# Tail products of four jobs on sixteen 32x32 tiles of TensorE at once, with the tails turned between partition quadrants by small SBUF copies

## Chip, cores and metric

The kernel runs on one core of one Trainium2 chip. The metric is the device time in microseconds (us); lower is better.

## The reference

```python
B, D, L = 16384, 416, 6                 # D = 26 * 16
# x0: (B, D), ws: (L, D, D), bs: (L, D), all bfloat16
def reference(x0, ws, bs):
    x = x0
    for l in range(L):
        proj = jnp.einsum('bd,de->be', x, ws[l]) + bs[l]
        x = x0 * proj + x
    return x
```

The rows are independent, so the kernel cuts them into 8 groups `g` of 2048 rows. One *job* is (g, l): one layer of one group. Its activations lie transposed in SBUF (the on-chip memory that the engines read), features on its 128 partitions. 416 features are three full tiles of 128 and a **tail** of 32. A row of the tail would waste three quarters of the 128 partitions, so the tail is folded: the 2048 rows are four chunks `j` of 512, and chunk j of the tail lies on partition quadrant j (partitions 32j to 32j+31) of one 128x512 tile.

## The kernel before

A job (g, l) makes 3 full output tiles (128 features x 2048 rows, 4 banks of PSUM, the memory in which TensorE sums) and one output tail (32 features x 4 chunks, one bank).

- `full`: 12 products 128x128, one per input tile and chunk.
- `rows32`: the contribution of the input tail to a full output tile. Four products with a contraction of only 32 rows, from the four quadrants, run side by side as tiles 32x128.
- `tails`: the output tails. The outputs have 32 features, so four products with 32 columns run side by side as tiles 128x32, one per chunk, each into its quadrant of the bank. The input tail's own share of the output tail would be 32x32; it is padded to 128 rows by a block-diagonal weight tile `wbd`.

```python
def rows32(g, l, i, banks, first):
    src, stok = x3_src(g, l)                              # the input tail, 128 x 512
    for j in range(NJ):
        q = slice(j * T32, (j + 1) * T32)
        ... matmul(bank(banks[j]), w3[l][q, ecols], src[q, :], tile_position=(j * T32, 0))

def tails(batch):                                         # up to four jobs, one bank each
    bs_ = take(len(batch))
    for (g, l), b in zip(batch, bs_):
        for t in range(NT):                               # three full input tiles
            for j in range(NJ):
                ... matmul(bank(b, j * T32, (j + 1) * T32), wm[l][:, t, NT * P:D], src(t, j, j + 1),
                           start=(t == 0), stop=False, tile_position=(0, j * T32))      # L449
        for j in range(NJ):                               # the input tail, padded
            ... matmul(bank(b, j * T32, (j + 1) * T32), wbd[l][:, j * T32:(j + 1) * T32], s3,
                       start=False, stop=True, tile_position=(0, j * T32))              # L454
        evacuate_tail(g, l, b)     # ScalarE: ts = psum + bias; VectorE: ts *= x0 tail; x3 = ts + old x3

def make_wbd(l):                                          # GpSimd builds the padding
    add("pool", memset(wbd[l], 0))
    for j in range(NJ): add("pool", tensor_copy(wbd[l][q, q], w3[l][q, NT * P:D]))
... # cut: loads, start, order of tiles, output, the last layer of the last group
```

Jobs run along antidiagonals of (g, l): a job's input comes from a job up to four places earlier (four for most jobs), and tails are made in batches. There are 47 tails in 14 batches: nine of four jobs, two of three, two of two and one of one. Each batch stands inside the stream of tiles.

## Time and profile before

| | before |
|---|---|
| time, median (range) | 487.95 us (487.85 to 488.16, 4 runs) |
| span, first to last instruction | 485.8 us |
| TensorE busy / VectorE / ScalarE | 99% / 84% / 71% |
| granted TensorE clock | 0.999 |
| TensorE waits for other engines, in all | 2.8 us |

The profile has its own short names: PE is TensorE, PEld its weight loads, DVE VectorE, ACT ScalarE, POOL GpSimd and SPq the queue of SyncE; L424 is line 424 of the kernel.

From the page of the kernel before: the span, the busy times, the chain that ended last by engine and by line, and the groups of the products and of the tails' VectorE add. Columns of a group are line, engine, operation, output and inputs, shape, count, then busy us and mean ns of one, then the idle time just before.

```profile
span 485.8 us, 8101 instructions
PE 478.7 (99%) x3253; PEld 203.4 (42%) x3253; DVE 407.8 (84%) x713; ACT 343.2 (71%) x372; POOL 16.5 (3%) x44
...
PE 96%; DVE 2%; ACT 1%; POOL 0%; issue 0%; POOLq 0%
...
L424 PE MATMUL ps<-x,wm 128*128 128x512 bf16 x1692 | 379.4, 380 | 0.0
...
L436 PE MATMUL ps<-x,w 32*128 32x512 bf16 x564 | 44.5, 380 | 1.0 <-DVE x L414 1.0
L449 PE MATMUL ps<-x,wm 128*32 128x512 bf16 x564 | 38.7, 380 | 0.0
...
L454 PE MATMUL ps<-x,wbd 128*32 128x512 bf16 x188 | 18.3, 379 | 0.0
```

The chain is TensorE almost alone, so the time is the sum of what TensorE has to issue. A matmul lasts 380 ns, but successive ones overlap: what counts is the distance of their starts. A busy TensorE therefore says nothing about how well its tiles are used. That is read from the timeline. The next lines are the timeline of TensorE in the kernel before, around one batch of four tails; columns are start (us), length (us), engine, line, operation and count.

```profile
158.80 0.40 PE L436 MATMUL ps<-x,w 32*128 32x512 bf16 x4
159.13 0.83 PE L449 MATMUL ps<-x,wm 128*32 128x512 bf16 x12
159.79 0.39 PE L454 MATMUL ps<-x,wbd 128*32 128x512 bf16 x4
160.00 0.82 PE L449 MATMUL ps<-x,wm 128*32 128x512 bf16 x12
160.65 0.39 PE L454 MATMUL ps<-x,wbd 128*32 128x512 bf16 x4
...
162.38 0.39 PE L454 MATMUL ps<-x,wbd 128*32 128x512 bf16 x4
162.70 0.60 PE L424 MATMUL ps<-x,wm 128*128 128x512 bf16 x2
```

From 160.00 to 160.65 there are 12 products in three rounds of four, 0.216 us a round; from 159.79 to 160.00 the padded L454 round costs as much as any other. The batch runs from 159.13 to 162.70: 3.57 us = 16 rounds x 0.216 + 0.11. The remainder 0.11 is at the end, where the tile shape changes from 128x32 to 128x128. It is the same at 158.80 to 159.13, where a round of 0.216 takes 0.33.

There is one more place where TensorE loses time, early on. Its timeline in the kernel before, near 24 us (the square bracket is idle time and what ended it):

```profile
23.15 0.40 PE L436 MATMUL ps<-x,w 32*128 32x512 bf16 x4
24.50 0.40 PE L436 MATMUL ps<-x,w 32*128 32x512 bf16 x4 [0.95 <-DVE x L414]
24.82 1.47 PE L424 MATMUL ps<-x,wm 128*128 128x512 bf16 x6
```

The second group of four reads the first tail that was computed, and has to wait for VectorE's add (L414) to write it.

### The profile page before, as it was taken

What the parts mean: (1) busy time and instruction counts of PE and PEld (TensorE: products, weight loads), DVE (VectorE), ACT (ScalarE), POOL (GpSimd) and SP (SyncE); (2) the same over time, 40 slices, a digit from 0 to 9 for tenths busy, and PEclk for the clock granted to TensorE, in tenths of its full rate; (3) what the DMA queues carried; (4) which work ended last, traced back from release to release, by engine and by line L of the source; (5) the groups of instructions that cost most, each with busy time, mean ns of one, the idle gap of its engine ahead of it and who ended that gap; (6) DMA issues with size and microseconds to landing.
All of it is one profiled execution on the core that took longest, in us unless ns stands there. A gap on an engine that the chain in (4) does not pass through costs nothing.

```text
span 485.8 us, 8101 instructions
## 1 busy us (share of the span) xinstructions
PE 478.7 (99%) x3253; PEld 203.4 (42%) x3253; DVE 407.8 (84%) x713; ACT 343.2 (71%) x372; POOL 16.5 (3%) x44
## 2 busy tenths in 40 slices
PE   8999999999999999999999999999999999999996
PEld 6344444444444444434444444444444444444353
DVE  2878888888888888888889888988888888888887
ACT  4567777677677676766777767767777767777775
POOL 1123000000000000000000000000000000000000
PEclk9999999999999999999999999999999999999999
DMA  8997860000002397269209911850000137027277
GB/s 228 203 186 168 169 139 1 0 1 0 2 1 43 67 239 119 45 149 229 46 13 203 227 24 36 214 175 1 1 1 1 24 67 193 0 45 169 73 160 260
DMA packets 126249, 47.65 MB, mean 98 GB/s; under 512 B 107002, under 2 KB 124804, under 8 KB 126212
## 3 DMA queue, kind: packets, MB, share of 16 engines
q1 hardware_dynamic: 125464, 46.60, 42.9%
q8 instruction: 25, 0.41, 0.4%
q10 hardware_dynamic: 748, 0.54, 0.3%
q14 instruction: 12, 0.10, 0.1%
HBM read 5.97 MB, written 13.63 MB: 40 GB/s over the span
## 4 chain that ended last, share of the span: by engine, by line
PE 96%; DVE 2%; ACT 1%; POOL 0%; issue 0%; POOLq 0%
PE ps L424 76%; PE ps L436 8%; PE ps L449 6%; PE ps L454 2%; PE ps L767 1%; PE ps L520 1%; PE ps L500 1%; DVE x L397 1%; ACT x L795 1%; DVE tw L392 1%; ACT x L759 0%; PE ps L525 0%; DVE x L802 0%; PE ps L778 0%; ACT tw L383 0%; PE ps L737 0%
## 5 line engine op out<-in xcount | busy, mean ns | idle before, releaser
L383 ACT ACTIVATE tw<-ps,bias 128x1024 bf16<-128x1024 f32 (+1 forms) x295 | 299.8, 1071 | 128.3 <-PE ps L436 104.5
L424 PE MATMUL ps<-x,wm 128*128 128x512 bf16 x1692 | 379.4, 380 | 0.0
L424 PEld LDWEIGHTS ps<-x,wm 128*128 128x128 bf16 x1692 | 158.9, 98 | 213.3 <-issue 28.5
L392 DVE TENSOR_TENSOR tw<-tw,x 128x1024 bf16<-128x1024 bf16 (+1 forms) x285 | 193.7, 685 | 62.9 <-ACT tw L383 62.5
L397 DVE TENSOR_TENSOR x<-tw,x 128x1024 bf16<-128x1024 bf16 (+1 forms) x285 | 182.6, 681 | 0.0
L436 PE MATMUL ps<-x,w 32*128 32x512 bf16 x564 | 44.5, 380 | 1.0 <-DVE x L414 1.0
L449 PE MATMUL ps<-x,wm 128*32 128x512 bf16 x564 | 38.7, 380 | 0.0
L410 ACT ACTIVATE ts<-ps,bias 128x512 bf16<-128x512 f32 x47 | 28.8, 700 | 0.0
L436 PEld LDWEIGHTS ps<-x,w 32*128 32x128 bf16 x564 | 9.1, 92 | 34.4 <-issue 33.1
L449 PEld LDWEIGHTS ps<-x,wm 128*32 128x32 bf16 x564 | 13.8, 96 | 15.7 <-issue 2.9
L609 POOL COPY ost<-ot 128x512 bf16<-128x512 bf16 x7 | 5.0, 717 | 412.9 <-DMA ot<-x 412.9
L414 DVE TENSOR_TENSOR x<-ts,x 128x512 bf16<-128x512 bf16 x47 | 18.5, 417 | 0.0
L412 DVE TENSOR_TENSOR ts<-ts,x 128x512 bf16<-128x512 bf16 x47 | 18.5, 417 | 0.0
L454 PE MATMUL ps<-x,wbd 128*32 128x512 bf16 x188 | 18.3, 379 | 0.0
L294 POOL COPY wbd<-w 32x32 bf16<-32x32 bf16 x24 | 9.3, 388 | 35.4 <-DMA w<-in_ws_dram 34.2
L767 PE MATMUL ps<-wm,x 128*128 128x416 bf16 x48 | 9.4, 341 | 0.0
L533 DVE COPY x<-ps 128x512 bf16<-128x512 bf16 x4 | 1.7, 424 | 8.6 <-PE ps L525 8.6
L795 ACT ACTIVATE x<-ps 128x416 bf16<-128x416 f32 x15 | 7.4, 530 | 1.3 <-PE ps L767 1.2
L530 ACT ACTIVATE x<-ps 128x512 bf16<-128x512 bf16 x8 | 4.3, 594 | 4.5 <-PE ps L520 4.5
L454 PEld LDWEIGHTS ps<-x,wbd 128*32 128x32 bf16 x188 | 5.0, 97 | 5.1
L767 PEld LDWEIGHTS ps<-wm,x 128*128 128x128 bf16 x48 | 5.1, 115 | 3.8 <-issue 1.4
L797 DVE TENSOR_TENSOR x<-x,x 128x416 bf16<-128x416 bf16 x15 | 5.5, 370 | 1.1 <-ACT x L795 1.0
(37 smaller groups left out, 49.7 us busy)
## 6 DMA issues: line engine op xcount, KB each, us to landing
out_dram<-ost SPq DMA_DIRECT2D x7, 1664.0 KB, 6.8
x<-in_x_dram SPq DMA_DIRECT2D x7, 416.0 KB, 7.5
wm<-in_ws_dram SPq DMA_DIRECT2D x5, 312.0 KB, 3.1
x<-Tb SPq DMA_DIRECT2D x28, 32.0 KB, 2.3
out_dram<-x SPq DMA_DIRECT2D x1, 832.0 KB, 3.6
w<-in_ws_dram SPq DMA_DIRECT2D x20, 26.0 KB, 2.2
x<-in_x_dram SPq DMA_DIRECT2D x2, 208.0 KB, 3.1
out_dram<-x SPq DMA_DIRECT2D x1, 416.0 KB, 2.5
```

The source lines that it names most:

```text
L383: add("act", lambda h, a=a, w=w, b0=b0: h.activation(tw[r][:, a * CH:(a + w) * CH], psum[:, b0 * CH:(b0 + w) * CH], ACT_F.Identity, bias=b ...
L392: add("dve", lambda h, a=a, e=e: h.tensor_tensor(tw[r][:, a * CH:e * CH], tw[r][:, a * CH:e * CH], x0s[s0][:, i * GC + a * CH:i * GC + e * ...
L397: add("dve", lambda h, a=a, e=e: h.tensor_tensor(xs[so][:, i * GC + a * CH:i * GC + e * CH], tw[r][:, a * CH:e * CH], src(i, a, e), ALU.ad ...
L410: add("act", lambda h: h.activation(ts[r][:, :], bank(b), ACT_F.Identity, bias=bias[:, 3, l:l + 1], scale=1.0), reads=[("ps", b), "bias"], ...
L412: add("dve", lambda h: h.tensor_tensor(ts[r][:, :], ts[r][:, :], x0s[s0][:, XW:XW + CH], ALU.mult), reads=[("ts", r)] + x03_toks(s0), writ ...
L414: add("dve", lambda h: h.tensor_tensor(x3s[so][:, :], ts[r][:, :], src, ALU.add), reads=[("ts", r)] + stok, writes=[("x3", so)], hold=True)
L424: add("pe", lambda h, t=t, j=j: h.matmul(bank(banks[j]), wm[l][:, t, ecols], src(t, j, j + 1), start=(first and t == 0), stop=(not first a ...
L436: add("pe", lambda h, q=q, j=j: h.matmul(bank(banks[j]), w3[l][q, ecols], src[q, :], start=first, stop=not first, tile_position=(j * T32, 0)),
L449: add("pe", lambda h, t=t, j=j, src=src, l=l, b=b: h.matmul(bank(b, j * T32, (j + 1) * T32), wm[l][:, t, NT * P:D], src(t, j, j + 1), star ...
L454: add("pe", lambda h, j=j, s3=s3, l=l, b=b: h.matmul(bank(b, j * T32, (j + 1) * T32), wbd[l][:, j * T32:(j + 1) * T32], s3, start=False, s ...
L767: add("pe", lambda h, t=t: h.matmul(bank(b, n=D), xcol(t, j, kk), wm[l][:, t, :], start=(first and t == 0), stop=(not first and t == NT - 1)),
L795: add("act", lambda h: h.activation(o, bank(b, n=D), ACT_F.Copy), reads=[("ps", b)], writes=extra + [("on", j, kk)])
```

## The change

The padded round does 32x32 of useful work in a 128x32 tile. The array can be cut in 16 tiles of 32x32, so the four padded rounds of a batch could be one round, **if the sixteen products of four jobs fall on sixteen distinct tiles**. Without more they do not: chunk j of every job lies on quadrant j and goes to quadrant j, so all jobs use the four diagonal tiles. The change therefore lets the tail of a group lie *turned*: for odd layers its chunks are moved by 0, 1, 1 or 2 quadrants according to g mod 4. Going from even to odd layers a job's product then moves by +0, +1, +1, +2 quadrants and from odd to even by -0, -1, -1, -2. Since neighbours in a batch differ by one in g and in l, four neighbours get the offsets 0, 1, 3 and 2, which are all different.

The price: `x3 = ts + old x3` needs the old tail in the new position. The new tail tile is filled beforehand with the turned old tail by two SBUF-to-SBUF DMAs, and the group's x0 tail gets a turned copy too. About 70 DMAs are added, all on the one queue (SyncE's) that also carries loads and outputs. `wbd` and its GpSimd work go. The early order of tiles changes too. To find memory for the turned copies, the transposed tail buffer `Tb` moves into the output buffer `ost`, and one temporary of the tails and a separate buffer of the biases are dropped. The core of the diff, cut:

```diff
-    NX0, NXS, NX3, NTW, NTS = 5, 6, 8, 4, 5
+    NX0, NXS, NX3, NTW, NTS = 5, 6, 10, 4, 4
...
-    def make_wbd(l): ...                               # and its calls
...
+        if turn_of(g, 1):                              # at the end of load_group
+            rotate(x0s[s][:, XW:XW + CH], x0s[s][:, XW + CH:XW + 2 * CH], turn_of(g, 1),
+                   x03_toks(s), ("x03r", s), f"x03r_{s}", g)
...
+    def turn_of(g, l):
+        return (0, 1, 1, 2)[g % 4] if l % 2 else 0
+    def quad(g, l, j):
+        q = (j + turn_of(g, l)) % NJ
+        return q, slice(q * T32, (q + 1) * T32)
+    def rotate(src, dst, n, reads, token, lane, batch):
+        a = P - n * T32
+        add("sp", lambda h: h.dma_start(dst[n * T32:P, :], src[0:a, :]), ...)
+        add("sp", lambda h: h.dma_start(dst[0:n * T32, :], src[a:P, :]), ...)
...
     def done_with(g, l):
...
+        prefill(g, l + 1)                              # turned copy of the old tail into the new
         if l == L - 1:
             output(g)
...
     def tails(batch):
         bs_ = take(len(batch))
+        for (g, l), b in zip(batch, bs_):
+            s3, tok3 = x3_src(g, l)
+            for j in range(NJ):
+                (ri, qi), (ro, qo) = quad(g, l, j), quad(g, l + 1, j)
+                add("pe", ... h.matmul(psum[qo, b * CH:(b + 1) * CH], w3[l][qi, NT * P:D], s3[qi, :],
+                    start=True, stop=False, tile_position=(ri * T32, ro * T32)), ...)
         for (g, l), b in zip(batch, bs_):
             for t in range(NT):
                 for j in range(NJ):
-                    ... matmul(bank(b, j * T32, (j + 1) * T32), ..., start=(t == 0), stop=False,
-                               tile_position=(0, j * T32))
+                    ... matmul(psum[qo, b * CH:(b + 1) * CH], ..., start=False, stop=(t == NT - 1),
+                               tile_position=(0, ro * T32))
-            for j in range(NJ):
-                ... matmul(bank(b, j * T32, (j + 1) * T32), wbd[l][:, j * T32:(j + 1) * T32], s3, ...)
...
-    where[((1, 0), 1)] = where.pop(((1, 0), 0))
-    tiles = [((1, 0), 0), ((0, 1), 0), ((1, 0), 1), ((0, 1), 1), ((0, 1), 2), ((1, 0), 2)]
+    where[((0, 1), 0)] = where.pop(((1, 0), 0))
+    tiles = [((1, 0), 0), ((1, 0), 1), ((0, 1), 0), ((0, 1), 1), ((0, 1), 2), ((1, 0), 2)]
```

More of the change, by code (lines that the diff above doesn't have):

```diff
@@ L234, in bass_standalone__cross_network_dcn__recsys_kernel @@
     w3 = [nc.alloc_sbuf_tensor(f"w3_{l}", [P, D], BF16) for l in range(L)]
-    wbd = [nc.alloc_sbuf_tensor(f"wbd_{l}", [P, P], BF16) for l in range(L)]
     ident = nc.alloc_sbuf_tensor("ident", [P, P], BF16)
     bias = nc.alloc_sbuf_tensor("bias", [P, 4, L], FP32)
-    bs_sb = nc.alloc_sbuf_tensor("bs_sb", [P, D], BF16)
     brow = nc.alloc_sbuf_tensor("brow", [P, D], BF16)
@@ L241, in bass_standalone__cross_network_dcn__recsys_kernel @@
     ones = nc.alloc_sbuf_tensor("ones", [P, P], BF16)
-    x0s = [nc.alloc_sbuf_tensor(f"x0_{s}", [P, XW + CH], BF16) for s in range(NX0)]
+    x0s = [nc.alloc_sbuf_tensor(f"x0_{s}", [P, XW + 2 * CH], BF16) for s in range(NX0)]
     xs = [nc.alloc_sbuf_tensor(f"x_{s}", [P, XW], BF16) for s in range(NXS)]
     x3s = [nc.alloc_sbuf_tensor(f"x3_{s}", [P, CH], BF16) for s in range(NX3)]
-    Tb = nc.alloc_sbuf_tensor("Tb", [P, GC], BF16)
     tw = [nc.alloc_sbuf_tensor(f"tw_{s}", [P, GC], BF16) for s in range(NTW)]
@@ L248, in bass_standalone__cross_network_dcn__recsys_kernel @@
     ost = nc.alloc_sbuf_tensor("ost", [P, GC // P, D], BF16)
+    Tb = ost[:, :, :].rearrange("p a f -> p (a f)")[:, 0:GC]
     ot3 = nc.alloc_sbuf_tensor("ot3", [P, KK, P], BF16)
@@ L261, in x0_all @@
     def x0_all(s):
-        return [x0_tok(s, t, j) for t in range(NT) for j in range(NJ)] + [("x03", s)]
+        return [x0_tok(s, t, j) for t in range(NT) for j in range(NJ)] + [("x03r", s), ("x03r", s, "b")]
     def x_all(s):
@@ L288, in load_w3 @@
                 writes=[("w3", l, j)], lane=f"w3{l}", batch=0)
-    def make_wbd(l):
-        add("pool", lambda h: h.memset(wbd[l][:, :], 0.0), writes=[("wbd", l)])
-        for j in range(NJ):
-            q = slice(j * T32, (j + 1) * T32)
-            add("pool", lambda h, q=q: h.tensor_copy(wbd[l][q, q], w3[l][q, NT * P:D]),
-                reads=[("w3", l, j)], writes=[("wbd", l)])
     def load_group(g, between=lambda: None):
@@ L305, in load_group @@
         turn(0)
-        add("sp", lambda h: h.dma_start_transpose(Tb[:, :], x0[rows, D - P:D]),
-            writes=["Tb"], lane="Tb", batch=g)
+        add("sp", lambda h: h.dma_start_transpose(Tb, x0[rows, D - P:D]),
+            writes=[("ost", t) for t in range(NT + 1)], lane="Tb", batch=g)
         turn(1)
@@ L313, in load_group @@
             add("sp", lambda h, q=q, j=j: h.dma_start(x0s[s][q, XW:XW + CH], Tb[P - T32:P, j * CH:(j + 1) * CH]),
-                reads=["Tb"], writes=[("x03q", s, j)], lane=f"x03_{s}", batch=g)
+                reads=[("ost", 0)], writes=[("x03q", s, j)], lane=f"x03_{s}", batch=g)
+        if turn_of(g, 1):
+            rotate(x0s[s][:, XW:XW + CH], x0s[s][:, XW + CH:XW + 2 * CH], turn_of(g, 1),
+                   x03_toks(s), ("x03r", s), f"x03r_{s}", g)
     def x03_toks(s):
         return [("x03q", s, j) for j in range(NJ)]
+    def turn_of(g, l):
[5 more added lines that the diff above has]
+        a = P - n * T32
+        add("sp", lambda h: h.dma_start(dst[n * T32:P, :], src[0:a, :]), reads=reads, writes=[token], lane=lane, batch=batch)
+        add("sp", lambda h: h.dma_start(dst[0:n * T32, :], src[a:P, :]), reads=reads, writes=[token + ("b",)],
+            lane=lane, batch=batch)
     tw_n, ts_n = [0], [0]
@@ L407, in evacuate_tail, with prefill @@
         ts_n[0] += 1
-        src, stok = x3_src(g, l)
-        so = xtail[(g, l + 1)]
+        if turn_of(g, l + 1):
+            x03, tok0 = x0s[s0][:, XW + CH:XW + 2 * CH], [("x03r", s0), ("x03r", s0, "b")]
+        else:
+            x03, tok0 = x0s[s0][:, XW:XW + CH], x03_toks(s0)
+        if l == 0:
+            so = free_3.pop(0)
+            xtail[(g, 1)] = so
+            res, rtok = x03, tok0
+        elif turn_of(g, 1):
+            so = xtail[(g, l + 1)]
+            res, rtok = x3s[so][:, :], [("x3", so), ("x3", so, "b")]
+        else:
+            so = free_3.pop(0)
+            xtail[(g, l + 1)] = so
+            res, rtok = x3_src(g, l)
         add("act", lambda h: h.activation(ts[r][:, :], bank(b), ACT_F.Identity, bias=bias[:, 3, l:l + 1], scale=1.0),
             reads=[("ps", b), "bias"], writes=[("ts", r)])
-        add("dve", lambda h: h.tensor_tensor(ts[r][:, :], ts[r][:, :], x0s[s0][:, XW:XW + CH], ALU.mult),
-            reads=[("ts", r)] + x03_toks(s0), writes=[("ts", r)], release=True)
-        add("dve", lambda h: h.tensor_tensor(x3s[so][:, :], ts[r][:, :], src, ALU.add),
-            reads=[("ts", r)] + stok, writes=[("x3", so)], hold=True)
+        add("dve", lambda h: h.tensor_tensor(ts[r][:, :], ts[r][:, :], x03, ALU.mult),
+            reads=[("ts", r)] + tok0, writes=[("ts", r)], release=True)
+        add("dve", lambda h: h.tensor_tensor(x3s[so][:, :], ts[r][:, :], res, ALU.add),
+            reads=[("ts", r)] + rtok, writes=[("x3", so), ("x3", so, "b")], hold=True)
+    def prefill(g, l):
+        if 0 < l < L and turn_of(g, 1) and (g, l) != (LAST, L - 1):
+            so = free_3.pop(0)
+            xtail[(g, l + 1)] = so
+            n = (turn_of(g, l + 1) - turn_of(g, l)) % NJ
+            rotate(x3s[xtail[(g, l)]], x3s[so], n, [("x3", xtail[(g, l)])], ("x3", so), f"rot{so}", (g, l))
     def full(g, l, i, banks, first, chunk_major, after_chunk=None, chunks=range(NJ)):
@@ L434, in rows32 @@
         for j in range(NJ):
-            q = slice(j * T32, (j + 1) * T32)
-            add("pe", lambda h, q=q, j=j: h.matmul(
+            r, q = quad(g, l, j)
+            add("pe", lambda h, q=q, j=j, r=r: h.matmul(
                 bank(banks[j]), w3[l][q, ecols], src[q, :], start=first, stop=not first,
-                tile_position=(j * T32, 0)),
-                reads=stok + [("w3", l, j)], writes=[("ps", banks[j])])
+                tile_position=(r * T32, 0)),
+                reads=stok + [("w3", l, r)], writes=[("ps", banks[j])])
@@ L441, in tails @@
     def tails(batch):
         bs_ = take(len(batch))
-        ready = []
+        for (g, l), b in zip(batch, bs_):
+            s3, tok3 = x3_src(g, l)
+            for j in range(NJ):
+                (ri, qi), (ro, qo) = quad(g, l, j), quad(g, l + 1, j)
+                add("pe", lambda h, l=l, b=b, s3=s3, ri=ri, qi=qi, ro=ro, qo=qo: h.matmul(
+                    psum[qo, b * CH:(b + 1) * CH], w3[l][qi, NT * P:D], s3[qi, :],
+                    start=True, stop=False, tile_position=(ri * T32, ro * T32)),
+                    reads=tok3 + [("w3", l, ri)], writes=[("ps", b)])
@@ L444, in tails @@
         for (g, l), b in zip(batch, bs_):
             src, stok = x_src(g, l)
-            s3, tok3 = x3_src(g, l)
             for t in range(NT):
                 for j in range(NJ):
-                    add("pe", lambda h, t=t, j=j, src=src, l=l, b=b: h.matmul(
-                        bank(b, j * T32, (j + 1) * T32), wm[l][:, t, NT * P:D], src(t, j, j + 1),
-                        start=(t == 0), stop=False, tile_position=(0, j * T32)),
+                    ro, qo = quad(g, l + 1, j)
+                    add("pe", lambda h, t=t, j=j, src=src, l=l, b=b, ro=ro, qo=qo: h.matmul(
+                        psum[qo, b * CH:(b + 1) * CH], wm[l][:, t, NT * P:D], src(t, j, j + 1),
+                        start=False, stop=(t == NT - 1), tile_position=(0, ro * T32)),
@@ L452, in tails @@
                         reads=[stok(t, j), ("wm", l)], writes=[("ps", b)])
-            for j in range(NJ):
-                add("pe", lambda h, j=j, s3=s3, l=l, b=b: h.matmul(
-                    bank(b, j * T32, (j + 1) * T32), wbd[l][:, j * T32:(j + 1) * T32], s3,
-                    start=False, stop=True, tile_position=(0, j * T32)),
-                    reads=tok3 + [("wbd", l)], writes=[("ps", b)])
-            xtail[(g, l + 1)] = free_3.pop(0)
             evacuate_tail(g, l, b)
@@ L471, in bass_standalone__cross_network_dcn__recsys_kernel @@
     nat = NX0 - 1
-    x0n = x0s[nat][:, :].rearrange("p (j k f) -> p j k f", j=NJ, k=KK)
+    x0n = x0s[nat][:, 0:XW + CH].rearrange("p (j k f) -> p j k f", j=NJ, k=KK)
     def perm(ap, j):
@@ L482, in bass_standalone__cross_network_dcn__recsys_kernel @@
     load_wm(0, "act")
-    add("act", lambda h: h.dma_start(bs_sb[0:L, :], bs[:, :]), writes=["bs_sb"], lane="bs", batch=0)
+    add("act", lambda h: h.dma_start(brow[0:L, :], bs[:, :]), writes=["brow"], lane="bs", batch=0)
     add("dve", lambda h: h.memset(warm[:, :], 0.0), writes=["warm"])
@@ L491, in bass_standalone__cross_network_dcn__recsys_kernel @@
     load_w3(0, "sp")
-    make_wbd(0)
     load_group(1, lambda: load_wm(1, "sp"))
@@ L546, in first_job @@
             add("pe", lambda h, t=t: h.transpose(
-                psum_t(bt)[:, t * 8:t * 8 + L], bs_sb[0:L, t * P:(t + 1) * P], ident[0:L, 0:L]),
-                reads=["bs_sb", "ident"], writes=[("ps", bt)])
+                psum_t(bt)[:, t * 8:t * 8 + L], brow[0:L, t * P:(t + 1) * P], ident[0:L, 0:L]),
+                reads=["brow", "ident"], writes=[("ps", bt)])
         for j in range(NJ):
@@ L551, in first_job @@
             add("pe", lambda h, j=j, q=q: h.matmul(
-                psum_t(bt)[q, NT * 8:NT * 8 + L], bs_sb[0:L, NT * P:D], ident[0:L, 0:L],
+                psum_t(bt)[q, NT * 8:NT * 8 + L], brow[0:L, NT * P:D], ident[0:L, 0:L],
                 is_transpose=True, tile_position=(0, j * T32)),
-                reads=["bs_sb", "ident"], writes=[("ps", bt)])
+                reads=["brow", "ident"], writes=[("ps", bt)])
         add("act", lambda h: h.activation(
@@ L565, in first_job @@
         load_w3(1, "act")
-        make_wbd(1)
-        make_wbd(2)
         full(g, l, 1, bb, True, True, chunks=[0, 1])
@@ L585, in bass_standalone__cross_network_dcn__recsys_kernel @@
     sn, so, s5 = slot(3), slot(4), slot(5)
-    x0n7, x5n, on = (x0s[s][:, :].rearrange(view, j=NJ, k=KK) for s in (sn, s5, so))
+    x0n7, x5n, on = (x0s[s][:, 0:XW + CH].rearrange(view, j=NJ, k=KK) for s in (sn, s5, so))
     rows7 = x0[LAST * GC:B, :]
@@ L595, in load_last @@
             add("sp", lambda h, j=j: h.dma_start(brow[j * T32:j * T32 + 1, :], bs[L - 1:L, :]),
-                writes=[("brow", j)], lane="brow", batch=0)
+                writes=[("brow", j)] + (["brow"] if j == 0 else []), lane="brow", batch=0)
     def output(g):
@@ L668, in start_job @@
             load_w3(W_LOAD[(g, l)], "sp")
-            make_wbd(W_LOAD[(g, l)])
         if (g, l) in G_LOAD:
@@ L727, in x3col @@
     def x3col(j, kk):
-        return s3[j * T32:(j + 1) * T32, :].rearrange("p (m k) -> p m k", k=KK)[:, :, kk]
+        return s3[quad(g, l, j)[1], :].rearrange("p (m k) -> p m k", k=KK)[:, :, kk]
     first_use = {"x5": True, "on": True}
@@ L743, in turn_tails @@
             for j in range(NJ):
-                q = slice(j * T32, (j + 1) * T32)
+                r, q = quad(g, l, j)
                 o = h2 * CH + NT * P
-                add("pe", lambda h, j=j, q=q, kk=2 * kp + h2, o=o: h.matmul(
+                add("pe", lambda h, j=j, q=q, r=r, kk=2 * kp + h2, o=o: h.matmul(
                     psum_t(bks[j])[:, o:o + T32], x3col(j, kk), ident[q, q], is_transpose=True,
-                    tile_position=(j * T32, 0)),
+                    tile_position=(r * T32, 0)),
                     reads=tok3 + ["ident"], writes=[("ps", bks[j])])
@@ L774, in nat_rows @@
             for j in range(NJ):
-                q = slice(j * T32, (j + 1) * T32)
+                r, q = quad(g, l, j)
                 st, sp_ = first and part == 0, not first and part == 1
                 if part == 0:
-                    add("pe", lambda h, j=j, q=q, st=st: h.matmul(
+                    add("pe", lambda h, j=j, q=q, r=r, st=st: h.matmul(
                         bank(bks[j], n=D), x3col(j, kk), w3[l][q, :], start=st, stop=False,
-                        tile_position=(j * T32, 0)),
-                        reads=tok3 + [("w3", l, j)], writes=[("ps", bks[j])])
-                else:
-                    add("pe", lambda h, j=j, sp_=sp_: h.matmul(
-                        bank(bks[j], n=D), ones[j * T32:j * T32 + 1, :], brow[j * T32:j * T32 + 1, :],
-                        start=False, stop=sp_, tile_position=(j * T32, 0)),
-                        reads=["ones", ("brow", j)], writes=[("ps", bks[j])])
+                        tile_position=(r * T32, 0)),
+                        reads=tok3 + [("w3", l, r)], writes=[("ps", bks[j])])
+                else:
+                    add("pe", lambda h, j=j, r=r, sp_=sp_: h.matmul(
+                        bank(bks[j], n=D), ones[r * T32:r * T32 + 1, :], brow[r * T32:r * T32 + 1, :],
+                        start=False, stop=sp_, tile_position=(r * T32, 0)),
+                        reads=["ones", ("brow", r)], writes=[("ps", bks[j])])
     def nat_mul(kk, j, b):
```

## The prediction

> **What bounds the kernel.** TensorE. The profile's first part has PE busy 99% of 485.8 us, and the chain that ended last is 96% PE: L424 (128x128 products) 76%, L436 (32-row products) 8%, L449 and L454 (tails) 6% and 2%. The clock is 0.999 and the waits show PE idle only 2.8 us: 1.8 us at the start and 0.95 us at L436 near 24 us, for the first tail's DVE add (L414). DVE (84%) and ACT (71%) have slack. So PE time removed is time saved, and little else counts.
>
> **What is removed.** In the trace of matmul starts, groups of four 32-column products start 0.216 us apart, the same as one 128x128 product. A four-job batch of tails is 16 such rounds (12 L449, 4 L454): 159.13 to 162.70 us, 3.57 us, of which 16 x 0.216 = 3.45 and about 0.11 is the change of tile shape at the end. The other changes I measured (128 to 32x128, 32x128 to 128x32) also cost 0.10 to 0.11 us over a round.
>
> After: the four L454 rounds of a batch become sixteen 32x32 products. The turns (0, 1, 1, 2) with signs by layer parity give the four jobs of a batch the offsets 0, 1, 3, 2, so all sixteen tiles are distinct. One block costs one round (0.216), a stagger of sixteen load-and-product pairs at 3.4 to 7 ns (trace: 3.4; 0.05 to 0.1 us), and one more shape change (0.11): about 0.38 us against 0.86. Savings, as an estimate: nine four-job batches x 0.48, two of three x 0.28, two of two x 0.08, one of one -0.12: 4.9 us. The cuts in batches of fewer jobs leave tiles empty, so the full 4x shows only in nine batches.
>
> The early reordering (both first tiles of (1,0) before (0,1)) should remove the 0.95 us wait on L414. Sum: 5.9 us.
>
> **What is added, off the path.** About 70 more SBUF-to-SBUF copies (like x<-Tb, 0.62 us issue each, 2.3 us to landing) on SP, in order behind outputs and group loads. The tight place: the load of the last group ends issuing at 281.9 us; its own turn must wait for landing (2.3) and issue (1.2), and only then the copies for job (3,5) issue, landing near 288.5. That job's tail add came at about 284.5. I expect DVE stalled here about 4 us, and under 1 us near 241. Four tw buffers and two tiles of PSUM should hide most of it; PE should lose 0 to 1 us. POOL loses the wbd work, which was off the path. Tb sharing ost costs nothing: the store lands within the preceding transpose's issue.
>
> **Prediction.** 487.98 - 5.9 + 0.3 = 482.4 us (about 1.1% faster), range 480.8 to 485.5. Faster by over 2%: 0.02; within 2%: 0.92; slower: 0.06.
>
> **What would show it.** Each four-job tail batch: first tail start to next 128x128 start falls from 3.57 to about 3.1 us. PE idle near 24 us gone. A DVE idle released by DMA near 280 to 288 us. L424 busy time unchanged.
>
> **What would make it wrong.** The Trainium skill, "TensorEngine Tiling (Array Packing)", Gotcha 1, says different row tiles cannot access the same PSUM bank simultaneously. Here the four products of one job come from four row tiles and write one bank, though on four partition quadrants. This trace shows row tiles only on different banks. If they are serialized, the block takes about four rounds (no saving, about 487) or sixteen (+3 us a batch, slower by some 6%). I take it that conflicts are per quadrant. "TensorE: Matmul & The Clock Gate", Part 3, gives 10.6x for sixteen tiles; no such pack is in this trace. A longer stagger, or late copies that stall PE, would cost 1 to 3 us.

## The result, and the profile after

The time after is 481.38 us (median of 4 runs, 481.07 to 481.85), against 487.95 us before. The ratio is 0.9866 with a 95% interval of 0.9849 to 0.9883: 1.3% faster, inside the predicted 480.8 to 485.5, and 1.0 us below the predicted 482.4. Ratios here and below are the mean time of one kernel's runs over the mean of the other's runs of the same rounds, so they are not quite the ratio of the medians quoted.

The same parts of the page of the changed kernel (line numbers have moved: L424 is now L456, L436 is L468, L449 is L488, and L479 are the new 32x32 products):

```profile
span 480.0 us, 8111 instructions
...
PE 467.7 (97%) x3199; PEld 199.8 (42%) x3253; DVE 406.5 (85%) x713; ACT 343.2 (72%) x372; POOL 7.0 (1%) x14
...
PE 94%; DMA 2%; ACT 1%; issue 1%; DVE 1%; SPq 0%
...
L456 PE MATMUL ps<-x,wm 128*128 128x512 bf16 x1638 | 371.9, 379 | 5.6 <-issue 4.0
...
L488 PE MATMUL ps<-x,wm 128*32 128x512 bf16 x564 | 33.0, 380 | 0.0
...
L479 PE MATMUL ps<-x,w 32*32 32x512 bf16 x188 | 6.0, 385 | 0.0
...
x<-x SPq DMA_DIRECT2D x24, 96.0 KB, 2.1
```

One trap: L456 counts 1638 products where L424 counted 1692, and TensorE seems to idle 4.0 us for "issue". Nothing was removed there: the weight loads (PEld) are 3253 in both, and 54 matmul records are missing from this trace. So busy times and idle of L456 must not be compared across the two pages; I use the starts of weight loads, which are complete. (The weight loads of these full products are 1692, busy for 158.9 us, on both pages.) The DMA line is one of three for the turning copies: 2.1 us from issue to landing.

The timeline of TensorE in the changed kernel around the same batch:

```profile
156.94 0.39 PE L468 MATMUL ps<-x,w 32*128 32x512 bf16 x4
157.27 0.43 PE L479 MATMUL ps<-x,w 32*32 32x512 bf16 x16
157.63 2.77 PE L488 MATMUL ps<-x,wm 128*32 128x512 bf16 x48
160.56 2.54 PE L456 MATMUL ps<-x,wm 128*128 128x512 bf16 x11 [0.16 <-issue]
```

All sixteen products of four jobs take from 157.27 to 157.63, and then come the 12 rounds of L488. The next full product is one of those not recorded (11 where 12 belong); its weight load starts at 160.33. So the batch lasts 160.33 - 157.26 = 3.07 us instead of 3.57.

And the early place, in the timeline of TensorE of the changed kernel:

```profile
23.80 0.61 PE L468 MATMUL ps<-x,w 32*128 32x512 bf16 x8
24.35 1.90 PE L456 MATMUL ps<-x,wm 128*128 128x512 bf16 x8
```

The eight row products stand together, and the wait is gone.

With the starts of the weight loads the two traces can be cut in 14 batches and the stretches between them, and the difference of the spans is accounted for:

| stretch | before, us | after, us | saved, us |
|---|---|---|---|
| first weight load to the first batch | 17.69 | 18.24 | -0.55 |
| one-job batch | 0.977 | 1.085 | -0.11 |
| first to second batch (early order) | 9.984 | 8.854 | 1.13 |
| two two-job batches, each | 1.841 | 1.746, 1.748 | 0.19 |
| two three-job batches, each | 2.704 | 2.407 | 0.59 |
| nine four-job batches, each | 3.567 | 3.068 | 4.49 |
| 12 other stretches between batches, all | | | within 0.01 |
| last batch to the last weight load | 23.32 | 23.32 | 0.00 |
| sum | | | 5.74 |

The spans differ by 5.8 us on the pages, 5.75 us in the traces. The stretch before the first weight load (1.78 us) and the one after the last (4.82 us) are equal in both. I do not count the first line as an effect of the change: it varied from 17.3 to 18.2 us over the twelve traces, the changed kernels and the two others alike (17.4 and 17.7 us in the two), and in the changed kernel's trace TensorE waits there for the DMA of the first rows (0.5 us in all), in the one before it does not. The medians, 6.57 us apart, agree with that: the other lines and the 0.33 us outside the span (experiment 9) make 6.62 us, with this line it would be 6.07. Without it the inside of the span gains 6.29 us. The batches give 5.16 of it and the early order 1.13.

The one new wait of size is VectorE's, among its waits in the changed kernel (total us, times, longest us):

```profile
DVE x L438 <- DMA x<-x: 3.5, 1, 3.5
```

It is the turned copy of job (3,5), behind the load of the last group in the queue, at 281.2 to 284.7 us: about the place and size that the prediction named. The smaller wait that it named near 241 us is not among the waits.

### The profile page after: what moved, and what is told of

Read it like the earlier page. It is cut to its first block, busy times and chain, and to the rows that moved or that the text cites. A ratio compares the mean times of both kernels' runs of the same rounds, so it can differ in the third digit from the quotient of the medians.

```text
span 480.0 us, 8111 instructions
## 1 busy us (share of the span) xinstructions
PE 467.7 (97%) x3199; PEld 199.8 (42%) x3253; DVE 406.5 (85%) x713; ACT 343.2 (72%) x372; POOL 7.0 (1%) x14
## 4 chain that ended last, share of the span: by engine, by line
PE 94%; DMA 2%; ACT 1%; issue 1%; DVE 1%; SPq 0%
PE ps L456 76%; PE ps L468 8%; PE ps L488 7%; DMA x<-in_x_dram 2%; PE ps L796 1%; PE ps L479 1%; ACT x L824 1%; ACT tw L394 0%; ACT x L788 0%; DVE x L831 0%; PE ps L807 0%; PE ps L552 0%; SPq L512 0%; DVE x L408 0%; PE ps L766 0%
## 5 line engine op out<-in xcount | busy, mean ns | idle before, releaser
L456 PE MATMUL ps<-x,wm 128*128 128x512 bf16 x1638 | 371.9, 379 | 5.6 <-issue 4.0
L456 PEld LDWEIGHTS ps<-x,wm 128*128 128x128 bf16 x1692 | 158.9, 98 | 213.5 <-issue 29.1
L468 PE MATMUL ps<-x,w 32*128 32x512 bf16 x564 | 44.4, 380 | 0.0
L488 PE MATMUL ps<-x,wm 128*32 128x512 bf16 x564 | 33.0, 380 | 0.0
L468 PEld LDWEIGHTS ps<-x,w 32*128 32x128 bf16 x564 | 9.1, 92 | 33.2 <-issue 33.1
L488 PEld LDWEIGHTS ps<-x,wm 128*32 128x32 bf16 x564 | 13.8, 96 | 15.5 <-issue 3.2
L436 DVE TENSOR_TENSOR ts<-ts,x 128x512 bf16<-128x512 bf16 x47 | 18.6, 419 | 0.0
L639 POOL COPY ost<-ot 128x512 bf16<-128x512 bf16 x7 | 6.1, 872 | 453.0 <-DMA ot<-x 453.0
L826 DVE TENSOR_TENSOR x<-x,x 128x416 bf16<-128x416 bf16 x15 | 5.5, 372 | 1.1 <-ACT x L824 0.9
L479 PE MATMUL ps<-x,w 32*32 32x512 bf16 x188 | 6.0, 385 | 0.0
L831 DVE TENSOR_TENSOR x<-x,x 128x416 bf16<-128x416 bf16 x16 | 5.6, 370 | 0.1
L532 PE MATMUL ps<-ident 128*128 128x128 bf16 x30 | 3.4, 290 | 1.8 <-POOL ident L501 1.8
```

Of the source, the lines that this page charges most:

```text
L436: add("dve", lambda h: h.tensor_tensor(ts[r][:, :], ts[r][:, :], x03, ALU.mult), reads=[("ts", r)] + tok0, writes=[("ts", r)], release=True)
L456: add("pe", lambda h, t=t, j=j: h.matmul(bank(banks[j]), wm[l][:, t, ecols], src(t, j, j + 1), start=(first and t == 0), stop=(not first a ...
L468: add("pe", lambda h, q=q, j=j, r=r: h.matmul(bank(banks[j]), w3[l][q, ecols], src[q, :], start=first, stop=not first, tile_position=(r * ...
L479: add("pe", lambda h, l=l, b=b, s3=s3, ri=ri, qi=qi, ro=ro, qo=qo: h.matmul(psum[qo, b * CH:(b + 1) * CH], w3[l][qi, NT * P:D], s3[qi, :], ...
L488: add("pe", lambda h, t=t, j=j, src=src, l=l, b=b, ro=ro, qo=qo: h.matmul(psum[qo, b * CH:(b + 1) * CH], wm[l][:, t, NT * P:D], src(t, j, ...
```

## Experiments

All ten gave correct results. "After" in the diffs is the changed kernel. Kernels sent together ran on one chip with the kernel before beside them (487.97, 487.70 and 487.78 us for experiments 1-4, 5-8 and 9-10). The changed kernel was not run again beside them, so comparisons with its 481.38 us are across runs; the ratios to the kernel before and the stretches of the traces are the firmer measure.

### 1. No turns: all jobs on the four diagonal tiles

```diff
     def turn_of(g, l):
-        return (0, 1, 1, 2)[g % 4] if l % 2 else 0
+        return 0
```

> The changed kernel with no job turned: all four jobs of a batch put their sixteen 32x32 products on the same four diagonal tiles, no turning copies are left, everything else stays. Theory A (the gain of a batch is four rounds packed into one because the sixteen tiles are distinct): the block of 32x32 products of a four-job batch goes from 0.36 to about 1.01 us (three more rounds of 0.216), a batch from 3.07 to 3.72 us, and over 33 added rounds the time rises by 7.1 us to about 488.5, level with or slightly above the kernel before. Rival B (the gain comes from smaller 32x32 products, from the removed GpSimd work or from grouping, not from distinct tiles): the time stays within 1 us of 481.4. Rival C (the copies cost something on the path): it rises by less than 7.1 us because they are gone.

Measured: 487.68 us, ratio 0.9997 (0.9984 to 1.0009): the gain is gone. The timeline of TensorE around the same batch in this kernel:

```profile
158.07 0.39 PE L468 MATMUL ps<-x,w 32*128 32x512 bf16 x4
158.40 1.04 PE L479 MATMUL ps<-x,w 32*32 32x512 bf16 x16
159.37 2.77 PE L488 MATMUL ps<-x,wm 128*32 128x512 bf16 x48
```

The block takes 0.97 us instead of 0.36; a four-job batch lasts 3.675 us, and the batches are 6.67 us longer in all than in the changed kernel. I had expected 7.1: three added rounds cost 0.606 rather than 0.647, because products of one round start one after the other (the *stagger*): sixteen starts take 0.050 us from first to last, four take 0.010. In the changed kernel the one round has sixteen starts; here the last of four rounds has only four, 0.04 us less. Rival B falls: smaller products, the removed GpSimd work and the grouping all remain here. What the early order (1.13 us) and the time outside the span (0.33 us, below) still gain is eaten by the batches, 1.51 us longer in all than before the change: a four-job batch by 0.11 us (3.675 against 3.567), one more change of tile shape. Rival C is not supported: what is missing to 7.1 us is missing inside the batches, and the stretches between them agree with the changed kernel's within 0.005 us although every copy is gone.

### 2. Two turns: two jobs share each tile

```diff
-        return (0, 1, 1, 2)[g % 4] if l % 2 else 0
+        return (0, 1, 0, 1)[g % 4] if l % 2 else 0
```

> Turns (0, 1, 0, 1) instead of (0, 1, 1, 2): two jobs of a four-job batch share each tile. Theory A: two rounds instead of one in nine four-job batches and in the two three-job batches, so a four-job batch takes 3.07 + 0.216 = 3.29 us and the time rises by 11 x 0.216 = 2.4 us to 483.8. Rival B: no change. If products were issued in an order that lets no two of the colliding jobs overlap with the others, three rounds are possible: 3.50 us a batch.

Measured: 483.39 us, ratio 0.9907 (0.9892 to 0.9923). In the timeline of TensorE:

```profile
157.72 0.62 PE L479 MATMUL ps<-x,w 32*32 32x512 bf16 x16
158.27 2.77 PE L488 MATMUL ps<-x,wm 128*32 128x512 bf16 x48
```

The block takes 0.55 us, and batches of four and of three are 0.19 us longer than in the changed kernel, 2.08 us in all (2.4 expected). One, two and four jobs per tile thus give blocks of 0.36, 0.55 and 0.97 us: the time follows the number of products that share a tile.

### 3. The block twice

```diff
-        for (g, l), b in zip(batch, bs_):
+        for (g, l), b, again in [(*p, r) for r in (0, 1) for p in zip(batch, bs_)]:
             s3, tok3 = x3_src(g, l)
...
-                    start=True, stop=False, tile_position=(ri * T32, ro * T32)),
+                    start=True, stop=not again, tile_position=(ri * T32, ro * T32)),
```

> The block of 32x32 products of every batch is issued twice (the second starts the sums anew, so the result is right). Theory A (a block is one round of 0.216 us, plus a short stagger and a change of tile shape that is paid once): each batch is 0.22 to 0.28 us longer, the time rises by 14 x 0.22 to 0.28 = 3.1 to 3.9 us to about 484.8. Rival D (row tiles that write one PSUM bank hinder each other, or dispatch of sixteen pairs is the limit, and the 0.36 us of the block is mostly that): each second block costs 0.36 us or more, 5 us or more in all.

Measured: 483.89 us, ratio 0.9920 (0.9908 to 0.9933). In the timeline of TensorE:

```profile
158.02 0.65 PE L479 MATMUL ps<-x,w 32*32 32x512 bf16 x32
158.60 2.77 PE L488 MATMUL ps<-x,wm 128*32 128x512 bf16 x48
```

Thirty-two products take 0.58 us, so the second sixteen cost 0.215 us, a plain round; over the 14 batches the second blocks add 3.0 us in the trace. (The medians differ by only 2.5 us, below the 3.1 to 3.9 expected; they come from separate rounds of runs, and single times vary by about 1 us.) Rival D falls. Each bank is written by four row tiles at the same time here, on four different quadrants, and this costs nothing that shows.

### 4 and 5. The early order alone, on both kernels

In experiment 4 the kernel before gets the new order, in experiment 5 the changed kernel the old one. The edit of 4 (5 is its reverse):

```diff
-    where[((1, 0), 1)] = where.pop(((1, 0), 0))
-    tiles = [((1, 0), 0), ((0, 1), 0), ((1, 0), 1), ((0, 1), 1), ((0, 1), 2), ((1, 0), 2)]
+    where[((0, 1), 0)] = where.pop(((1, 0), 0))
+    tiles = [((1, 0), 0), ((1, 0), 1), ((0, 1), 0), ((0, 1), 1), ((0, 1), 2), ((1, 0), 2)]
```

> The kernel before with only the early order of tiles of the change (two tiles of job (1,0) ahead of the first of (0,1), tails after it). Theory A: the 0.95 us wait of TensorE for the first tail's add near 24 us goes and one change of tile shape with it, 1.1 us in all: 486.8. Rival E (the start gained because loads and GpSimd work fell away, not by the order): within 0.3 us of the kernel before, 487.9.

> The changed kernel with the early order of tiles of the kernel before. Theory A: the wait near 24 us comes back, +1.1 us: 482.5. Rival E: no change, 481.4.

Measured: experiment 4 took 486.76 us, ratio 0.9978 (0.9966 to 0.9991); experiment 5 took 482.49 us, ratio 0.9891 (0.9878 to 0.9903). In the traces the stretch from the first to the second batch is 8.852 us in experiment 4, as in the changed kernel, and 9.830 us in experiment 5. The wait is back in the timeline of TensorE in experiment 5:

```profile
24.46 0.40 PE L468 MATMUL ps<-x,w 32*128 32x512 bf16 x4 [0.80 <-DVE x L438]
```

So theory A holds and rival E falls: the order alone makes this part of the gain, on either kernel, 1.13 and 0.98 us. It is independent of the packing and could have been had without it. The size of 1.1 us was expected for a wrong reason, though: no change of tile shape goes away (both groups of row products have the same shape); what the 0.95 us lacks is explained under point 3 of the account below.

### 6, 7, 8 and 10. How late may the turned copy be?

These move the one copy that VectorE waits for. Experiment 6 issues the load of the last group one job later, so that the copy of (3,5) goes ahead. Experiments 7, 10 and 8 repeat the turning copy of the last group's x0 tail 1, 3 and 4 times, which holds the queue up and makes the copy of (3,5) later.

```diff
# 6
         prefill(g, l + 1)
+        if later:
+            load_group(later.pop())
...
-                load_group(g + NX0)
+                if g == 2:
+                    later.append(g + NX0)
+                else:
+                    load_group(g + NX0)
# 7, 10, 8: n = 1, 3, 4, at the end of load_group
+            for k in range(n if g == LAST else 0):
+                rotate(x0s[s][:, XW:XW + CH], x0s[s][:, XW + CH:XW + 2 * CH], turn_of(g, 1),
+                       x03_toks(s), ("x03r", s), f"x03r_{s}", (g, k))
```

> The load of the last group is issued one job later, so that the turning copy of job (3,5) goes ahead of it. Theory F (the 3.5 us that VectorE waits for that copy near 281 us is hidden by free buffers): the VectorE wait for a DMA disappears from the waits and the time stays at 481.4 within 0.2. Rival G (that wait delays TensorE by up to 1 us, as the prediction allowed): 480.4 to 481.0.

> The turning copy of the last group's x0 tail is done once more (waiting for the first to land), so the copy of (3,5) behind it lands about 3.3 us later. Theory F: VectorE waits about 7 us there, TensorE loses nothing, since ScalarE has four buffers (four tiles, about 11 us of evacuation) to fill: 481.4 within 0.2. Rival G: +1 to +3 us.

> Three further repeats of the last group's turning copy, between one (5.0 us of VectorE wait, nothing lost) and four (12.3 us, 2 to 7 us lost). Theory F: VectorE waits about 10 us, ScalarE fills its fourth buffer at about the time the first comes free, TensorE does not wait and the clock stays full: 481.1 within 0.3. Rival J (the loss grows with the wait from the start and is only small at one repeat): 482.5 to 485.

> The same copy done four times more: the copy of (3,5) lands about 13 us later and VectorE waits about 17 us. Theory F: the four buffers are full after about 10 to 11 us, then two tiles of PSUM after about 3 us more, so TensorE stalls here for about 2 to 5 us: 483.5 to 486. If nothing is lost, the slack is larger than I work out; if the whole 17 us show, there is none.

| | VectorE waits for the copy, us | time, us | ratio to before (95%) | later start of the next batch, us |
|---|---|---|---|---|
| 6, copy ahead | 0 | 481.11 | 0.9864 (0.9851 to 0.9877) | 0.00 |
| changed kernel | 3.5 | 481.38 | 0.9866 (0.9849 to 0.9883) | |
| 7, one repeat | 5.0 | 481.11 | 0.9865 (0.9852 to 0.9878) | 0.00 |
| 10, three repeats | 10.6 | 481.73 | 0.9874 (0.9859 to 0.9889) | 0.64 |
| 8, four repeats | 12.3 | 487.73 | 0.9987 (0.9958 to 1.0016) | 4.04 |

The last column compares the stretch before the tenth batch with the changed kernel's, in the traces. Up to 5.0 us of wait TensorE loses nothing in this stretch, so the copies are hidden as they stand (theory F; rival G falls). The times alone could not decide it: both medians of 481.11 us lie just outside what either side had named, by less than the spread of the runs. At 10.6 us it begins to: theory F had expected none there, and the trace shows 0.64 us, while the times of experiment 10 do not separate from the others. Rival J, a loss that grows from the start, is not what is seen. The waits of VectorE were expected at about 7, 10 and 17 us and came out at 5.0, 10.6 and 12.3: each repeat lengthened the wait by 1.5 to 2.4 us, not by 3.3.

Experiment 8 was a miss in size. It waits less than expected and yet loses more than the 483.5 to 486 us expected: a median of 487.73, with single times from 483.47 to 488.58, against 481.11 us of experiment 7 on the same chip. In its profiled run (485.81 us) the timeline of TensorE shows only about 2 us of waits for ScalarE:

```profile
296.85 0.61 PE L459 MATMUL ps<-x,wm 128*128 128x512 bf16 x2 [1.61 <-ACT tw L397]
297.86 1.72 PE L459 MATMUL ps<-x,wm 128*128 128x512 bf16 x4 [0.40 <-ACT tw L397]
299.80 2.08 PE L459 MATMUL ps<-x,wm 128*128 128x512 bf16 x5 [0.22 <-issue]
```

(The 0.22 for "issue" is a missing record: its weight load, at 299.37, is in the trace.) From start to start, less the 0.216 us of a plain product, the two gaps cost 1.77 and 0.56 us, 2.33 in all. That is 1.69 us more than the 0.64 of experiment 10, and VectorE's wait is 1.7 us longer: beyond a slack of about 10 us TensorE seems to wait one for one (two points only).

The rest of the 4.04 us is the clock. The windows view of the same run gives, for each stretch, its length, the busy times and counts of the five engines' rows, and then the granted clock:

```profile
297.00:298.00 1.00, 0.60 (x3) 0.11 (x2) 1.00 (x3) 0.80 (x1) 0.00 (x0) 1.00 0.00 0
298.00:301.00 3.00, 2.78 (x7) 1.03 (x7) 3.00 (x7) 2.12 (x2) 0.00 (x0) 0.51 0.00 0
301.00:302.00 1.00, 1.00 (x7) 0.27 (x9) 1.00 (x3) 0.00 (x0) 0.00 (x0) 0.76 0.00 0
302.00:303.00 1.00, 1.00 (x11) 0.31 (x4) 1.00 (x3) 0.70 (x1) 0.00 (x0) 1.00 0.00 0
```

After the two gaps the clock is halved for about 3.4 us, in which products start 0.427 us apart instead of 0.216; this costs 1.7 us. The profiled run has a mean clock of 0.995, the one at 483.47 us has 0.998, within the 0.998 to 1.000 of every other run here. The four runs above 487 us have 0.992 to 0.995. A clock that dropped for longer can be a part of what they lose beyond the profiled run, but not all: one of them, 1.6 us longer, has the same 0.995, and 0.003 less over 485 us is about 1.5 us where the others are over 2 us longer. They have no trace, so this stays open.

### 9. The GpSimd work put back

```diff
+    wbd = [nc.alloc_sbuf_tensor(f"wbd_{l}", [P, P], BF16) for l in range(3)] * 2
...
+    def make_wbd(l): ...            # as in the kernel before, and its four calls
```

> The changed kernel with the GpSimd work of the kernel before put back (30 small instructions that build block-diagonal tiles nobody reads; three tiles instead of six, since memory is short). The sums inside the span explain 6.3 us of the gain when starts are equal; the times show some 0.3 us more between the time and the span: 2.1 to 2.2 us outside the span for the kernel before and its reordered version, 1.8 us for every changed version. Theory H (the GpSimd work lengthens the launch or the end outside the span by 0.3 us): 481.7, with 2.15 us outside the span. Rival I (something else does, such as the size of the program): 481.4, with 1.8 us outside. Neither expects a change inside the span.

Measured: 481.58 us, ratio 0.9875 (0.9858 to 0.9891). The stretches of the trace agree with the changed kernel's within 0.003 us, the start and the time after the last weight load (0.02 us) left aside, so the GpSimd work was off the path, as it seemed. Time minus span is 2.02 to 2.11 us in its four runs, against 1.83 to 1.87 for the changed kernel and 2.16 to 2.20 for the kernel before on the same chip. So putting this work back costs about 0.2 us of the 0.33 us outside the span (0.27 of 0.39 if experiment 10, on the same chip with 1.76 to 1.84 us, is taken as the changed kernel); the rest is open, and so is the way in which it does this, since the profile shows nothing outside the span. The number of instructions alone, rival I's example, is not it: experiment 3 has 376 more than the changed kernel, on TensorE, and stays at 1.77 to 1.89 us. In the times themselves 0.2 us does not separate.

## Why the prediction was right

The time lay inside the range, and each step can be held against the traces.

1. **TensorE's issue is the time.** Right. VectorE and ScalarE do the same work as before, and a gain inside TensorE's stream came out whole: 6.29 us of gain in the stretches, none given back.
2. **Four padded rounds become one block of about 0.38 us.** Right, at 0.365 us. The sum over the batches was predicted as 4.9 us and is 5.16. The block was put about 0.015 us too high: sixteen starts take 0.050 us (3.3 ns a step, the low end of the range that I gave), of which a plain round already contains 0.010. The other few thousandths of a microsecond per batch are rounding in my sum. Experiments 1 and 2 show that the distinct tiles make the gain and not the smaller products. The predicted loss of 0.12 us in the one-job batch was there too (0.108): one round stays one round, and a change of tile shape is added.
3. **The early order removes 0.95 us.** Right in mechanism, undersized: 1.13 us. The idle of 0.95 us that the profile gives counts from the modelled end of the matmul before, and that end lies 0.40 us after its start (23.15), while a next round could have started after 0.216 us. The idle time thus understates the gap by about 0.18 us (in experiment 5 too: 0.80 us of idle, 0.98 us lost). In a pipelined stream a wait should be read from start to start.
4. **The copies are hidden.** Right: VectorE waits 3.5 us (about 4 predicted), TensorE nothing. I had allowed 0.3 us for it in the sum, and none was lost; experiment 6 shows that removing the wait gains nothing that can be seen.
5. **Row tiles on one bank.** This was named as what could make the prediction wrong: the Trainium skill, "TensorEngine Tiling (Array Packing)", Restrictions and Gotchas, Gotcha 1, has different row tiles unable to access one PSUM bank at a time. Here they do, on different quadrants: sixteen more products cost 0.215 us (experiment 3), no more than one round. That conflicts are per quadrant was a guess when the prediction was made, since no trace then showed such a case; it was the guess on which the gain of the packing hung.
6. **Not foreseen:** the 0.33 us outside the span, of which experiment 9 gives about 0.2 to the GpSimd work that I had called free.

With the terms as measured, 487.95 - 5.16 - 1.13 - 0.33 = 481.33 us, against a median of 481.38. The 1.0 us between prediction and median is, but for rounding, the sum of four small terms on the same side: 0.26 (batches), 0.18 (order), 0.3 (allowance for copies) and 0.33 (outside the span).

## What to carry to other kernels

When TensorE is the limit, count rounds, start to start, and ask of each whether its tiles are full; busy time hides a padded product completely. Small products pack only if their tiles are distinct, so it can pay to move *data* between quadrants, with copies on a queue that has room for them, to make them so; each batch that packs nothing pays a change of tile shape for it (here 0.11 us). A late copy is free only up to a limit that buffers set: here 5 us cost nothing, 10.6 us began to show, and at 12.3 us TensorE's waits (2.3 us) were followed by a halved clock, which cost another 1.7 us in the run that was traced.

## What the Trainium skill lacked or had wrong

- "TensorEngine Tiling (Array Packing)", Restrictions and Gotchas, Gotcha 1: "Different row tiles cannot access same PSUM bank simultaneously" is too wide. Four row tiles wrote each of four banks at once, on distinct quadrants, at full rate (0.215 us for sixteen products, experiment 3) and with right results. Row tiles that write the same quadrant of one bank were not tried.
- The same page, Tiling Modes, Key Properties, says that changing the tiling mode drains TensorE and gives no cost. The traces fit this and show 0.10 to 0.11 us over a plain round for each change read here.
- "TensorE: Matmul & The Clock Gate", Why this matters for your kernels, asks for no idle gaps of TensorE above about 3 us. In experiment 8 two gaps of 1.61 and 0.40 us within 3 us were followed by half the clock for about 3.4 us, so keeping to that row is not enough; this is one profiled run.
- "SBUF — State Buffer", SBUF: two separate sides, describes an exclusive lock between VectorE operations with two SBUF inputs and GpSimd, and gives no sense of how long it can last when VectorE is full. In experiments 7, 8 and 10, where VectorE worked off its backlog with almost no gap, one GpSimd copy of 128x512 took 5.7, 22.3 and 27.6 us; the other six copies in each of these runs took 0.6 to 1.1 us. That fits the page, but the lock itself is not in the trace, and in experiments 7 and 10 the copy ended while VectorE still showed no gap, so what let it end is open.
- No page has the cost of GpSimd work outside the span: 0.2 to 0.3 us for 30 small instructions (experiment 9).
